# Four block pairs of a first projection by Strassen's seven products, with a ring of eight PSUM banks

## The chip, the core and the metric

The kernel runs on one core of one Trainium2 chip. The metric is the device time of one launch in microseconds (us), median of the runs. PE is TensorE (matmuls), DVE is VectorE, ACT is ScalarE, POOL is GpSimd, SP is the engine that issues most of the stores. PSUM is the memory that PE writes[...]. SBUF is the working memory.

## What is computed

Sparse attention of 8 batches with 8 heads, 576 positions and 64 values a head (four heads see the last 32 positions, four see every 32nd), followed by a bilinear feed-forward part on the 4608 resulting rows of 512 values:

```python
a = x @ w_a                      # 4608 x 512 by 512 x 1536
b = x @ w_b
return (a * b @ w_out)           # 4608 x 1536 by 1536 x 512
```

## The kernel before

Matmuls take bf16 operands and add up in f32. The 4608 rows are cut into nine tiles of 512. `xT` holds the attention output transposed, with the 512 values of a row in `KD` = 4 slices of 128 partitions. The 1536 middle columns are `FD` = 12 blocks of 128.

The work is a list of slots, 16 for each tile. Slots 0 to 11 of a tile are `ffn_ab(t, f)`, the first projection of block f: four matmuls (one per slice, 512 columns each) for `a` and four for `b`, all of them line 581, each group into a PSUM bank of its own. ACT copies `a` to SBUF (line 598), and DVE multiplies it by `b`, which it reads from PSUM, into `pf` (lines 601 and 603). Slots 12 to 15 are the output projection. For tiles 2 to 8 this is already done by Strassen's seven products (`y_plan`, for tile 8 `y_tail`): a two by two block matrix product with seven multiplications in place of eight, for which DVE makes sums of blocks of `pf` beforehand (`fast_s`, lines 614, 616, 618), and sums of blocks of `w_out` once (`fast_w`). The products are the matmuls of lines 686 and 714 (256 columns each). Products that share a bank letter in the plan go into one bank one after the other, the later one added to the earlier one; between them ACT or DVE reads the bank. The last subtraction of each quarter is done by POOL (line 881 for tiles 2 to 7; lines 730 and 735 for tile 8).

The order is written by hand. [...] Attention steps of a later batch lie between the slots of tiles 0 to 6; the last, `V7` of batch 7, is at slot 110. `do(slot, f, ...)` appends work after a slot: loads, `fast_s`, the POOL subtractions, the stores. After a slot that has such work, POOL first makes a one-element copy of that slot's result (`pace`, line 936), which holds POOL's queue back until the slot is done. The sums of a tile's `pf` are spread in this way over the slots of its projection; for tile 8 the sums of pair g (blocks 2g and 2g+1) stand after slot 2g+1.

`mm_bank` hands out PSUM banks in turn. From slot 0 on, the pools are `pst` (two banks, attention scores), `o` (two, attention output), and three `mm` banks with one `tp` bank, which make a ring of four for the projections. Tile 8's output products take the freed `o` and `pst` banks for their second half.

Of the kernel before, what the change touches and what calls it, by code (L numbers as in the profile page):

```python
# [7 lines left out]
F32 = mybir.dt.float32  # L8
BF16 = mybir.dt.bfloat16
I16 = mybir.dt.int16  # L10
ALU = mybir.AluOpType
# [13 lines left out]
VW = 128  # L25
WCH = (0, 2, 5, 9, 12)
FAST_Y = (2, 3, 4, 5, 6, 7, 8)


@with_exitstack  # L30
def kernel(
# [10 lines left out]
    nc = tc.nc  # L42
    B, H, S, D = q.shape
# [5 lines left out]
    KD = d_model // 128  # L49
    FD = d_ff // 128  # L50
    TTOK = 512
    NT = n_tok // TTOK
# [5 lines left out]
    nat = ctx.enter_context(tc.tile_pool(name="nat", bufs=1))  # L58
    sb = ctx.enter_context(tc.tile_pool(name="sb", bufs=3))
    fsb = ctx.enter_context(tc.tile_pool(name="ffn", bufs=2))  # L60
    pst = ctx.enter_context(tc.tile_pool(name="pst", bufs=1, space=bass.MemoryType.PSUM))
    dram = ctx.enter_context(tc.tile_pool(name="dram", bufs=2, space=bass.MemoryType.DRAM))

    psum4 = {}

    def open_psum(stack, **bufs):
        for nm, n in bufs.items():
            psum4[nm] = stack.enter_context(tc.tile_pool(name=f"p{nm}", bufs=n, space=bass.MemoryType.PSUM))
# [7 lines left out]
    def qk_buf(nm):  # L76
        return (const.tile([128, 2, S], BF16, name=f"{nm}l"), const.tile([128, 2, RS * GP], BF16, name=f"{nm}s"))

    qz_buf = [[qk_buf(f"qz{i}{j}") for j in range(2)] for i in range(2)]
    kT_buf = [(const.tile([128, 2, PAD + S], BF16, name=f"kT{i}l"), const.tile([128, 2, RS * GP + 48], BF16, name=f"kT{i}s"))  # L80
              for i in range(2)]
    vl_buf = [const.tile([128, HL * 6, VW], BF16, name=f"vl{i}") for i in range(2)]

    nat_s = {nm: const.tile([128, 3, RS * D], BF16, name=f"nat{nm}") for nm in "qk"}
    p_buf = [const.tile([128, 2, PW], BF16, name=f"p{i}") for i in range(5)]
# [72 lines left out]
    XR = 4  # L158
    xT = const.tile([128, KD, XR * S], BF16)
    wa_sb = wp.tile([128, KD, d_ff], BF16)  # L160
    wb_sb = wp.tile([128, KD, d_ff], BF16)
    wo_sb = wp.tile([128, FD, d_model], BF16)

    FG = FD // 2
    HT = TTOK // 2
    SW = HT + 16
    HN = d_model // 2
# [391 lines left out]
    def take(pos):  # L559
        for b, names in steps.get(pos, ()):  # L560
            run(b, names)

    pfs = {}

    used = [0]

    def mm_bank(shape):
        nm = "tp" if used[0] % 4 == 3 and used[0] >= 0 else "mm"
        used[0] += 1
        return psum4[nm].tile(shape, F32, tag=nm, name="mm")  # L570

    def ab_mm(t, f, ab, kks, mid=None, first=0, last=KD - 1, ws=(0, 1)):
        n = min(TTOK, XR * S - TTOK * t % (XR * S))
        cuts = [(0, n)] + ([(n, TTOK - n)] if n < TTOK else [])
        for w, ps_ in [((wa_sb, wb_sb)[i], ab[i]) for i in ws]:
            if mid and ps_ is ab[1]:
                mid()
            for kk in kks:
                for c0, n in cuts:
                    x0 = (TTOK * t + c0) % (XR * S)  # L580
                    nc.tensor.matmul(ps_[:, c0:c0 + n], lhsT=w[:, kk, 128 * f:128 * (f + 1)], rhs=xT[:, kk, x0:x0 + n],  # L581
                                     start=(kk == first and c0 == 0), stop=(kk == last and c0 == cuts[-1][0]))

    def ffn_ab(t, f, mid, ab=None):
        if f == 0:
            pfs[t] = fsb.tile([128, FD, TTOK], BF16, tag="pf", name="pf", bufs=1)
        pf = pfs[t]
        if ab is None:
            ab = [mm_bank([128, TTOK]) for _ in range(2)]
            if f == 0:  # L590

                late = 1 if t == 1 else 3
                ab_mm(t, f, ab, [kk for kk in range(KD) if kk != late], last=-1)
                ab_mm(t, f, ab, [late], first=-1, last=late)
            else:
                ab_mm(t, f, ab, range(KD), mid)
        a_sb = fsb.tile([128, TTOK], F32, tag="a_sb", name="a_sb")
        nc.scalar.copy(a_sb, ab[0])  # L598
        if t in FAST_Y:
            halves = lambda x: x.rearrange("p (a i s) -> p a i s", i=2, s=16)  # L600
            nc.vector.tensor_mul(pf[:, f, :].rearrange("p (i a s) -> p a i s", i=2, s=16), halves(a_sb), halves(ab[1]))  # L601
        else:
            nc.vector.tensor_mul(pf[:, f, :], a_sb, ab[1])  # L603
        return pf[:1, f, :1]
# [87 lines left out]
    def y_tail(t):  # L692

        plan, y = products(t), y_bufs()
        w, e = f32t("ya"), f32t("ye")
        v = {"a": w, "y": y}
        for q in range(2):
            if q == 0:
                bank = {x: mm_bank([128, HN]) for x in "abcd"}
            else:  # L700
                bank = {"a": psum4["o"].tile([128, 2, 512], F32, tag="o", name="end")[:, 0, :HN],
                        "b": pst.tile([128, 2, 512], F32, tag="st", name="end")[:, 0, :HN],
                        "c": mm_bank([128, HN]), "d": mm_bank([128, HN])}
            c21, c12, c22 = y[1][:, q, col(0)], y[0][:, q, col(1)], y[1][:, q, col(1)]
            wq, eq = w[:, q], e[:, q]
            seen = set()
            for k in ("3415267", "3412567")[q]:
                b, lhs, rhs = plan[k]
                cuts = [(slice(0, HN), bank[b])]
                if (k, q) == ("7", 1):  # L710
                    cuts = [(slice(0, 128), bank[b][:, :128]), (slice(128, HN), mm_bank([128, 128]))]
                for n, dst in cuts:
                    for g in range(FG):
                        nc.tensor.matmul(dst, lhsT=lhs(g, q), rhs=rhs(g)[:, n], start=g == 0 and b not in seen,  # L714
                                         stop=g == FG - 1, skip_group_check=True)
                        if g < FG - 1:
                            yield v
                    if k == "3":
                        nc.scalar.copy(wq, bank["a"])
                    elif k == "4":  # L720
                        nc.vector.tensor_tensor(wq, bank["b"], wq, op=ALU.add)
                        if q == 0:
                            fast_s(t, 1, slice(FG - 1, FG))
                    elif k == "1":
                        nc.vector.tensor_tensor(eq, bank["c"], wq, op=ALU.add)
                        if q == 0:
                            fast_s(t, 2, slice(FG - 1, FG))
                    elif k == "2":
                        nc.scalar.copy(c21, bank["b"])
                        nc.gpsimd.tensor_tensor(wq, wq, c21, op=ALU.subtract)  # L730
                        if q == 1:
                            y_store(nc.sync, t, y, 1, q, col(0))
                    elif k == "5":
                        nc.scalar.copy(c12, bank["a"])
                        nc.gpsimd.tensor_tensor(eq, eq, c12, op=ALU.subtract)
                        if q == 1:
                            y_store(nc.scalar, t, y, 0, q, col(1))
                    elif k == "6":
                        nc.vector.tensor_tensor(c22, bank["c"], wq, op=ALU.add)
                        y_store(nc.sync, t, y, 1, q, col(q) if q else slice(0, d_model))  # L740
                    else:
                        nc.vector.tensor_tensor(y[0][:, q, n], eq[:, n], dst, op=ALU.subtract)
                        if q == 0:
                            y_store(nc.sync, t, y, 0, q)
                        else:
                            y_store(nc.scalar if n.start == 0 else nc.sync, t, y, 0, q, n)
                    yield v
                seen.add(b)
# [48 lines left out]
    with tc.manual_schedule(engines={ENG.PE, ENG.SP, ENG.Pool, ENG.DVE, ENG.Activation}):  # L797
# [30 lines left out]
        for nm in ORDER:  # L828
            if nm[0] == "*":
                spin(int(nm[1:]))  # L830
            elif nm == "C0":
                for x, cp, n in ((raw[0], nc.vector.tensor_copy, "k"), (raw[1], nc.scalar.copy, "q")):
                    t = nats[0, n, False][:, 0:2].rearrange("p h r d -> p (h r d)")
# [21 lines left out]
            elif nm[0] == "F":  # L855
                f = int(nm[1])
# [10 lines left out]
            else:  # L867
                PART[nm[:-2] + nm[-1]](int(nm[-2]))
        early.close()
        open_psum(ctx, mm=3, tp=1, o=1)  # L870
        slots = []
        for t in range(NT):
            slots += [(ffn_ab, t, f) for f in range(FD)] + [(ffn_ys if t in FAST_Y else ffn_y, t, j) for j in range(4)]
# [4 lines left out]
        at = {}  # L878

        def do(i, fn, *args):  # L880
            at.setdefault(i, []).append(lambda: fn(*args))

        soon = {16 * t + 11: [lambda t=t: fast_s(t, 0, slice(2, 6))] for t in FAST_Y[:-1]}
        do(0, fill_v, vl_buf[0])
# [34 lines left out]
            do(slot, fast_w, n, slice(3, 6))  # L919
        for g in range(FG):  # L920
            for n in range(3 if g < FG - 1 else 1):
                do(16 * (NT - 1) + 2 * g + 1, fast_s, NT - 1, n, slice(g, g + 1))
        for t in FAST_Y[:-1]:
            for slot, n, z0, z1 in ((4, 0, 0, 2), (6, 2, 0, 2), (8, 1, 0, 2), (10, 2, 2, 4), (11, 2, 4, 6),
                                    (12, 1, 2, 6)):
                do(16 * t + slot, fast_s, t, n, slice(z0, z1))
        for i, (fn, t, j) in enumerate(slots):
            if i == 0:
                used[0] = -1000 * 3
            elif i == 16:  # L930
                used[0] = 0
            mid = lambda: take(i - 0.5)
            done = fn(t, j, mid) if fn is not ffn_ab else fn(t, j, mid, first.get(j) if t == 0 else None)
            if i > 13 and i in at and done is not None:

                nc.gpsimd.tensor_copy(pace, done)  # L936
            for f in soon.get(i, ()):
                f()
            take(i)
            for f in at.get(i, ()):  # L940
                f()
# [28 lines left out]
```

## Time and profile before

| | |
|---|---|
| device time, median of 3 runs | 328.78 us (328.7 to 328.8) |
| span of the profiled run | 326.3 us, mean PE clock 0.999 |
| tile 7: projection, output products | 262.6 to 283.4, 283.4 to 292.5 us |
| tile 8: projection, output products and end | 292.5 to 313.2, 313.2 to 326.3 us |
| VectorE busy in these four stretches | 10.5 of 20.8, 5.2 of 9.1, 14.2 of 20.7, 4.9 of 13.1 us |
| ScalarE busy in them | 7.0, 1.8, 7.0, 2.2 us |
| GpSimd busy in them | 4.8, 2.4, 3.4, 3.1 us |

The page of a profile gives the busy time of each engine, the span in 40 slices with a digit for each engine (9 is busy for 90% or more), the chain of work that ended last followed back from the end, and groups of instructions by line. A timeline row gives the start in us, the duration in us, engine, line, operation, output and inputs, the shape, and in brackets how long the engine was idle before and what it waited for. A chain row gives start, duration, engine, line and how many instructions in a row.

### The profile page before, as it was taken

Reading aid. Unit: us, or ns where it says so; the run is one execution under the profiler, and the core shown is the slowest. Engines: PE = TensorE matmul, PEld = TensorE weight load, DVE = VectorE, ACT = ScalarE, POOL = GpSimd, SP = SyncE. Lnnn points to the kernel's source line nnn. Section 1 sums busy time; section 2 is a strip of 40 time slices with the busy share of each in tenths; the row PEclk is TensorE's granted clock in tenths of the full one; section 3 lists DMA queues with packets and bytes.
Section 4 is the critical chain, followed back from the end, with each engine's and each line's share of the span. In section 5 each row is a group of like instructions: output and inputs, shape, how many; then the busy total and the mean of one; then the engine's idle time right before and its main releaser. Section 6 shows DMA issues by size and latency. Waiting matters only on the chain.

```text
span 326.3 us, 7676 instructions
## 1 busy us (share of the span) xinstructions
PE 320.6 (98%) x2820; PEld 205.5 (63%) x2820; DVE 265.7 (81%) x509; ACT 202.7 (62%) x329; POOL 177.2 (54%) x295
## 2 busy tenths in 40 slices
PE   8999999999999999999999999999999999999995
PEld 6754655455555587557999985569555954584474
DVE  6766888889778999999999999999877845647562
ACT  6764775478778765777677757875677643313321
POOL 8935839599966655875577557853312031232021
PEclk9999999999999999999999999999999999999999
DMA  9999999999999798799979999898033022004004
GB/s 151 154 204 201 204 184 182 173 171 136 132 213 116 95 97 79 77 217 125 83 72 199 138 86 77 160 180 84 20 77 115 2 67 64 0 2 129 1 2 129
DMA packets 98869, 37.50 MB, mean 115 GB/s; under 512 B 76688, under 2 KB 96016, under 8 KB 98832
## 3 DMA queue, kind: packets, MB, share of 16 engines
q0 software_dynamic: 85968, 19.48, 64.5%
q1 hardware_dynamic: 12576, 17.34, 18.4%
q8 instruction: 22, 0.36, 0.4%
q10 hardware_dynamic: 288, 0.20, 0.2%
q14 instruction: 15, 0.12, 0.1%
HBM read 39.51 MB, written 9.44 MB: 150 GB/s over the span
## 4 chain that ended last, share of the span: by engine, by line
PE 96%; DMA 2%; POOL 0%; DVE 0%; issue 0%; POOLq 0%; ACT 0%; DVEq 0%
PE mm L581 56%; PE mm L686 17%; PE mm L768 6%; PE st L385 5%; PE o L486 4%; DMA shared<-in_q_dram 2%; PE mm L714 2%; PE o L442 1%; PE ab L581 1%; PE misc L154 1%; PE tp L511 1%; PE tp L296 1%; PE end L714 1%; PE tp L287 0%; POOL shared L197 0%
## 5 line engine op out<-in xcount | busy, mean ns | idle before, releaser
L581 PE MATMUL mm<-xT,wa_sb 128*128 128x512 bf16 (+1 forms) x472 | 110.3, 357 | 0.0
L581 PE MATMUL mm<-xT,wb_sb 128*128 128x512 bf16 (+1 forms) x472 | 110.3, 357 | 0.0
L598 ACT COPY a_sb<-mm 128x512 f32<-128x512 f32 x106 | 62.1, 586 | 48.3 <-PE mm L581 47.6
L936 POOL CAST pace<-pf 1x1 f32<-1x1 bf16 x84 | 31.4, 374 | 84.0 <-DVE pf L601 80.7
L581 PEld LDWEIGHTS <-wb_sb 128*128 128x128 bf16 x480 | 46.3, 98 | 44.0 <-issue 0.2
L601 DVE TENSOR_TENSOR pf<-a_sb,mm 128x512 bf16<-128x512 f32 x84 | 56.4, 672 | 17.0 <-PE mm L581 13.8
L581 PEld LDWEIGHTS <-wa_sb 128*128 128x128 bf16 x480 | 42.7, 98 | 31.3
L393 ACT ACTIVATE p<-st 128x576 bf16<-128x576 f32 (+1 forms) x64 | 41.6, 650 | 11.7 <-PE st L385 11.1
L495 ACT ACTIVATE xr<-o 64x576 f32<-64x576 f32 x48 | 31.1, 649 | 25.0 <-PE o L486 24.2
L686 PEld LDWEIGHTS <-ps 128*128 128x128 bf16 x360 | 34.6, 98 | 3.9
L496 ACT ACTIVATE xr<-xr 64x576 f32<-64x576 f32 x48 | 32.9, 685 | 1.5
L500 DVE TENSOR_TENSOR xT<-o,xr 64x288 bf16<-64x288 f32 x48 | 21.5, 447 | 7.2 <-ACT xr L496 6.7
L502 DVE TENSOR_TENSOR xT<-o,xr 64x288 bf16<-64x288 f32 x48 | 21.5, 448 | 6.2 <-ACT xr L496 5.1
L686 PE MATMUL mm<-wf,ps 128*128 128x256 bf16 x216 | 26.4, 273 | 0.0
L768 PE MATMUL mm<-wo_sb,pf 128*128 128x512 bf16 x96 | 23.4, 379 | 0.0
L403 DVE TENSOR_TENSOR p<-p,mask_l 128x576 int16<-128x576 int16 x32 | 22.2, 694 | 1.2 <-ACT p L393 1.1
L243 POOL DMA_DIRECT2D vs<-in_v_dram x24 | 19.7, 821 | 3.0 <-PE st L385 2.2
L212 POOL DMA_DIRECT2D kl<-in_k_dram x24 | 16.1, 671 | 5.5 <-issue 3.6
L212 POOL DMA_DIRECT2D ql<-in_q_dram x24 | 16.0, 666 | 5.2 <-DMA wo_sb<-in_moe_w_out_dram 3.8
L603 DVE TENSOR_TENSOR pf<-a_sb,mm 128x512 bf16<-128x512 f32 x22 | 14.9, 676 | 4.3 <-ACT a_sb L598 2.8
L936 POOL COPY pace<-y_sb 1x1 f32<-1x1 f32 x16 | 2.8, 177 | 27.8 <-ACT y_sb L669 15.1
L686 PE MATMUL mm<-wf,pf 128*128 128x256 bf16 x144 | 17.6, 273 | 0.0
(162 smaller groups left out, 502.1 us busy)
## 6 DMA issues: line engine op xcount, KB each, us to landing
out_dram<-y_sb SPq DMA_DIRECT2D x12, 512.0 KB, 4.6
out_dram<-y_sb SPq DMA_DIRECT2D x10, 256.0 KB, 3.3
vl<-in_v_dram POOLq DMA_DIRECT2D x6, 384.0 KB, 6.8
kl<-in_k_dram POOLq DMA_DIRECT2D x24, 72.0 KB, 3.0
ql<-in_q_dram POOLq DMA_DIRECT2D x24, 72.0 KB, 3.0
vs<-in_v_dram POOLq DMA_DIRECT2D x24, 72.0 KB, 3.7
wo_sb<-in_moe_w_out_dram POOLq DMA_DIRECT2D x4, 384.0 KB, 9.2
natk<-in_k_dram POOLq DMA_DIRECT2D x20, 72.0 KB, 3.3
```

The source lines that it names most:

```text
L212: nc.gpsimd.dma_start(out=t[32 * h:32 * h + 32], in_=src[b, h].rearrange("(i y) d -> y i d", y=32))
L393: nc.scalar.activation(p[:M, :, :W], st[:M, :, :W], ACT.Exp, scale=scale)
L403: nc.vector.tensor_tensor(pi, pi, mk, op=ALU.bitwise_and)
L495: nc.scalar.activation(r, sums, ACT.Ln)
L496: nc.scalar.activation(r, r, ACT.Exp, scale=-1.0)
L500: nc.vector.tensor_mul(dst[:, W * half:W * (half + 1)], o[:64, j, :W], r[:, j])
L581: nc.tensor.matmul(ps_[:, c0:c0 + n], lhsT=w[:, kk, 128 * f:128 * (f + 1)], rhs=xT[:, kk, x0:x0 + n], start=(kk == first and c0 == 0), sto ...
L598: nc.scalar.copy(a_sb, ab[0])
L601: nc.vector.tensor_mul(pf[:, f, :].rearrange("p (i a s) -> p a i s", i=2, s=16), halves(a_sb), halves(ab[1]))
L686: nc.tensor.matmul(bank[b][:, q], lhsT=lhs(g, q), rhs=rhs(g), start=new and q == 0 and g == 0, stop=g == FG - 1, skip_group_check=True)
L768: nc.tensor.matmul(ybank[j], lhsT=pf[:, f, 128 * j:128 * (j + 1)], rhs=wo_sb[:, f], start=(f == 0), stop=(f == FD - 1))
L936: nc.gpsimd.tensor_copy(pace, done)
```

## The change

For the pairs g = 1 and g = 3 (blocks 2 and 3, 6 and 7) of tiles 7 and 8, the factor `a` is computed by Strassen's seven products instead of eight matmuls of 512 columns: the two blocks of a pair, the two halves of the 512 rows (interleaved by 16 rows) and the two halves of the 512 input values make the two by two blocks. The factor `b` stays as it was. The purpose is to have fewer matmul columns.

The sums of blocks of `w_a` (`fast_aw`) are made by VectorE in slots 104 to 110, those of `xT` (`fast_ax`) in slots 111 and 112 for tile 7 and 124 to 127 for tile 8. They and the f32 intermediates lie in buffers of the attention part, which are free by then. Inside a pair PE's order is products 3, 4, 1, 7, the `b` block of the first member, products 2, 5, 6, the `b` block of the second. The two multiplications into `pf` are owed: they are written behind the next block's work.

From tile 7 on (slot 112) the four pools of PSUM end, and one ring of eight banks takes their place; POOL's pacing copies stop there too. In the second half of tile 8's output the last subtractions go from POOL to VectorE, which reads the product from its bank. The sums of tile 8's `pf` are moved to slots 1, 4, 5, 8, 9 and 11.

```diff
+FAST_A = {7: (1, 3), 8: (1, 3)}
...
+    def fast_ax(t, n):
+        (j, i), (j2, i2), op = (((0, 0), (1, 1), ALU.add), ((0, 1), (1, 1), ALU.subtract), ((1, 0), (0, 0), ALU.subtract),
+                                ((0, 0), (0, 1), ALU.add), ((1, 0), (1, 1), ALU.add))[n]
+        nc.vector.tensor_tensor(xsum[t % 2][n].rearrange("p k (a s) -> p k a s", s=16), xhalf(t, j, i), xhalf(t, j2, i2), op=op)
...
+        plan = {"3": ("a", wav[:, 0, 0, g], xs[1]), "4": ("b", wav[:, 1, 1, g], xs[2]), "1": ("c", asum[0][:, g], xs[0]),
+                "7": ("d", asum[4][:, g], xs[4]), "2": ("b", asum[1][:, g], xhalf(t, 0, 0)),
+                "5": ("a", asum[2][:, g], xhalf(t, 1, 1)), "6": ("c", asum[3][:, g], xs[3])}
+        for k in ("3", "4", "1", "7", 0, "2", "5", "6", 1):
+            if k not in plan:
+                bank[k] = direct(2 * g + k)
+                continue
+            b, lhs, rhs = plan[k]
+            new = b not in bank
+            if new:
+                bank[b] = mm_bank([128, HT])
+            for kk in range(2):
+                nc.tensor.matmul(bank[b], lhsT=lhs[:, kk], rhs=rhs[:, kk], start=new and kk == 0, stop=kk == 1,
+                                 skip_group_check=True)
+            if k == "3":
+                nc.scalar.copy(w, bank["a"])
+            elif k == "4":
+                nc.vector.tensor_tensor(w, bank["b"], w, op=ALU.add)
+            elif k == "1":
+                nc.vector.tensor_tensor(v, bank["c"], w, op=ALU.add)
+            elif k == "7":
+                nc.vector.tensor_tensor(v, bank["d"], v, op=ALU.add)
+                while owed:
+                    owed.pop(0)()
+            elif k == "2":
+                nc.scalar.copy(c(1, 0), bank["b"])
+            elif k == "5":
+                nc.scalar.copy(c(0, 1), bank["a"])
+                nc.gpsimd.tensor_tensor(c(0, 0), v, c(0, 1), op=ALU.subtract)
+            else:
+                nc.vector.tensor_tensor(w, bank["c"], w, op=ALU.add)
+                nc.gpsimd.tensor_tensor(c(1, 1), w, c(1, 0), op=ALU.subtract)
+        owed.extend((lambda: product(0), lambda: product(1)))
...
+        if f // 2 in FAST_A.get(t, ()):
+            if f % 2 == 0:
+                fast_a(t, f // 2)
+            return None
+        while owed:
+            owed.pop(0)()
...
                         nc.scalar.copy(c21, bank["b"])
-                        nc.gpsimd.tensor_tensor(wq, wq, c21, op=ALU.subtract)
-                        if q == 1:
+                        if q == 0:
+                            nc.gpsimd.tensor_tensor(wq, wq, c21, op=ALU.subtract)
+                        else:
+                            nc.vector.tensor_tensor(wq, wq, bank["b"], op=ALU.subtract)
                             y_store(nc.sync, t, y, 1, q, col(0))
...
-        open_psum(ctx, mm=3, tp=1, o=1)
+        open_psum(mid_psum, mm=3, tp=1, o=1)
...
-                do(16 * (NT - 1) + 2 * g + 1, fast_s, NT - 1, n, slice(g, g + 1))
+                do(16 * (NT - 1) + (1, 4, 5, 8, 9, 11)[g], fast_s, NT - 1, n, slice(g, g + 1))
...
+        for t, when in ((7, (111, 111, 112, 112, 112)), (8, (124, 125, 126, 127, 127))):
+            for n, slot in enumerate(when):
+                do(slot, fast_ax, t, n)
...
+            elif i == 112:
+                used[0] = -1000 * 3
+                mid_psum.close()
+                open_psum(late_psum, mm=8)
...
-            if i > 13 and i in at and done is not None:
+            if 13 < i < 112 and i in at and done is not None:
```

More of the change, by code (lines that the diff above doesn't have):

```diff
@@ L60 @@
     fsb = ctx.enter_context(tc.tile_pool(name="ffn", bufs=2))
-    pst = ctx.enter_context(tc.tile_pool(name="pst", bufs=1, space=bass.MemoryType.PSUM))
+    mid_psum, late_psum = ctx.enter_context(ExitStack()), ctx.enter_context(ExitStack())
+    pst = mid_psum.enter_context(tc.tile_pool(name="pst", bufs=1, space=bass.MemoryType.PSUM))
     dram = ctx.enter_context(tc.tile_pool(name="dram", bufs=2, space=bass.MemoryType.DRAM))
@@ L582, in ab_mm @@
                                      start=(kk == first and c0 == 0), stop=(kk == last and c0 == cuts[-1][0]))
+    wav = wa_sb.rearrange("p (j k) (g e m) -> p j e g k m", j=2, e=2, m=128)
+    flat = lambda x: x.rearrange("p a b -> p (a b)")
+    asum = [flat(x)[:, 1536 * z:1536 * (z + 1)].rearrange("p (g k m) -> p g k m", g=FG, k=2)
+            for x, z in ((vl_buf[0], 0), (vl_buf[0], 1), (vl_buf[1], 0), (vl_buf[1], 1), (nat_s["k"], 0))]
+    xsum = [[flat(qz_buf[i][x][y])[:, 512 * z:512 * (z + 1)].rearrange("p (k m) -> p k m", k=2)
+             for x, y, z in ((0, 0, 0), (0, 0, 1), (0, 1, 0), (0, 1, 1), (1, 0, 0))] for i in range(2)]
@@ new lines, with xhalf, fast_aw @@
+    scratch = [flat(p)[:, :2 * HT].bitcast(F32) for p in p_buf[:4]]
+    def xhalf(t, j, i):
+        x0 = TTOK * t % (XR * S)
+        return xT[:, 2 * j:2 * j + 2, x0:x0 + TTOK].rearrange("p k (a i s) -> p i k a s", i=2, s=16)[:, i]
+    def fast_aw(n, gs):
+        (j, e), (j2, e2), op = (((0, 0), (1, 1), ALU.add), ((0, 1), (1, 1), ALU.add), ((0, 0), (1, 0), ALU.add),
+                                ((0, 1), (0, 0), ALU.subtract), ((1, 0), (1, 1), ALU.subtract))[n]
+        nc.vector.tensor_tensor(asum[n][:, gs], wav[:, j, e, gs], wav[:, j2, e2, gs], op=op)
@@ new lines, in fast_ax, with fast_a, direct, product @@
+    def fast_ax(t, n):
+        (j, i), (j2, i2), op = (((0, 0), (1, 1), ALU.add), ((0, 1), (1, 1), ALU.subtract), ((1, 0), (0, 0), ALU.subtract),
+                                ((0, 0), (0, 1), ALU.add), ((1, 0), (1, 1), ALU.add))[n]
+        nc.vector.tensor_tensor(xsum[t % 2][n].rearrange("p k (a s) -> p k a s", s=16), xhalf(t, j, i), xhalf(t, j2, i2), op=op)
+    owed = []
+    def fast_a(t, g):
+        pf, xs = pfs[t], xsum[t % 2]
+        a = [flat(x)[:, :2 * TTOK].bitcast(F32) for x in kT_buf[g % 2]]
+        c = lambda e, i: a[e][:, HT * i:HT * (i + 1)]
+        w, v = scratch[2 * (g % 2)], scratch[2 * (g % 2) + 1]
+        bank = {}
+        def direct(f):
+            b = mm_bank([128, TTOK])
+            x0 = TTOK * t % (XR * S)
+            for kk in range(KD):
+                nc.tensor.matmul(b, lhsT=wb_sb[:, kk, 128 * f:128 * (f + 1)], rhs=xT[:, kk, x0:x0 + TTOK], start=kk == 0,
+                                 stop=kk == KD - 1)
+            return b
+        def product(e):
+            f, b = 2 * g + e, bank[e]
+            nc.vector.tensor_mul(pf[:, f, :].rearrange("p (i a s) -> p i a s", i=2, s=16),
+                                 a[e].rearrange("p (i a s) -> p i a s", i=2, s=16),
+                                 b.rearrange("p (a i s) -> p i a s", i=2, s=16))
+        plan = {"3": ("a", wav[:, 0, 0, g], xs[1]), "4": ("b", wav[:, 1, 1, g], xs[2]), "1": ("c", asum[0][:, g], xs[0]),
[31 more added lines that the diff above has]
+        owed.extend((lambda: product(0), lambda: product(1)))
@@ L697, in y_tail @@
         for q in range(2):
[L698 to L703, printed above, removed]
+            bank = {x: mm_bank([128, HN]) for x in "abcd"}
             c21, c12, c22 = y[1][:, q, col(0)], y[0][:, q, col(1)], y[1][:, q, col(1)]
@@ L734, in y_tail @@
                         nc.scalar.copy(c12, bank["a"])
-                        nc.gpsimd.tensor_tensor(eq, eq, c12, op=ALU.subtract)
-                        if q == 1:
+                        if q == 0:
+                            nc.gpsimd.tensor_tensor(eq, eq, c12, op=ALU.subtract)
+                        else:
+                            nc.vector.tensor_tensor(eq, eq, bank["a"], op=ALU.subtract)
                             y_store(nc.scalar, t, y, 0, q, col(1))
@@ L926 @@
                 do(16 * t + slot, fast_s, t, n, slice(z0, z1))
+        for slot, n, g in ((104, 0, 1), (104, 1, 1), (105, 2, 1), (105, 3, 1), (106, 4, 1), (107, 0, 3), (108, 1, 3), (109, 2, 3), (109, 3, 3), (110, 4, 3)):
+            do(slot, fast_aw, n, slice(g, g + 1))
+        for t, when in ((7, (111, 111, 112, 112, 112)), (8, (124, 125, 126, 127, 127))):
+            for n, slot in enumerate(when):
+                do(slot, fast_ax, t, n)
         for i, (fn, t, j) in enumerate(slots):
```

## The prediction

> **What bounds the kernel now.** I read the page first: busy shares, slices, then the chain that ended last.
>
> ```profile
> PE 320.6 (98%) x2820; PEld 205.5 (63%) x2820; DVE 265.7 (81%) x509; ACT 202.7 (62%) x329; POOL 177.2 (54%) x295
> PE   8999999999999999999999999999999999999995
> PE 96%; DMA 2%; POOL 0%; DVE 0%; issue 0%; POOLq 0%; ACT 0%; DVEq 0%
> ```
>
> PE is busy in every slice but the last, and 96% of the chain is PE. A busy PE need not be PE at its peak, so I asked next for PE's waits from 232 us to the end (the answer has no row) and for the chain in order of time over the end:
>
> ```profile
> 283.36 9.17 PE mm L686 x84
> 292.52 20.72 PE mm L581 x96
> ...
> 320.58 0.38 ACT y_sb L729
> 320.96 0.07 issue
> 321.03 0.73 POOL ya L730
> 321.76 0.70 POOLq L965
> 322.45 0.02 issue
> 322.48 0.29 DVE y_sb L742
> ```
>
> The first projection of tile 8 is 96 matmuls of 512 columns in 20.72 us, **0.2158 us each**; the output products of tile 7 are 84 of 256 columns in 9.17 us, **0.1092 us each**. Both stream without a gap. Hence any matmul time saved in tiles 7 and 8 comes off the end, and any wait put in front of a matmul there is added. Only the last part, from 320.55 us, is a chain of copies, subtractions and stores.
>
> So the question is whether the helpers keep up. The VectorE timeline at the start of tile 8 shows how its queue runs:
>
> ```profile
> 296.09 0.69 DVE L601 TENSOR_TENSOR pf<-a_sb,mm 128x512 bf16<-128x512 f32 x1 [0.65 <-PE mm L581]
> 296.81 0.29 DVE L614 TENSOR_TENSOR ps<-pf 128x256 bf16<-128x256 bf16 x1
> 297.02 1.62 DVE L616 TENSOR_TENSOR ps<-pf 128x512 bf16<-128x512 bf16 x1
> 298.56 0.41 DVE L618 TENSOR_TENSOR ps<-pf 128x512 bf16<-128x512 bf16 x1
> ...
> 300.26 0.29 DVE L614 TENSOR_TENSOR ps<-pf 128x256 bf16<-128x256 bf16 x1
> 300.47 0.42 DVE L616 TENSOR_TENSOR ps<-pf 128x512 bf16<-128x512 bf16 x1
> 300.81 0.42 DVE L618 TENSOR_TENSOR ps<-pf 128x512 bf16<-128x512 bf16 x1
> 301.27 0.69 DVE L601 TENSOR_TENSOR pf<-a_sb,mm 128x512 bf16<-128x512 f32 x1
> ```
>
> It runs in written order: the product of a block, three sums of the same block pair (0.97 us in all), then the next product. The third row takes 1.62 us instead of 0.42. In the POOL timeline its neighbour is
>
> ```profile
> 297.10 1.26 POOL L881 TENSOR_TENSOR y_sb<-ya,y_sb 128x512 f32<-128x512 f32 x1
> ```
>
> which ends at 298.36, just before the VectorE sum does. Today this delay hides: block f's banks are wanted again only two blocks later.
>
> [...] 1.62 against 0.42 us above, while L601, with a PSUM input, ran its usual 0.69 us at 267.92 beside L881 (267.16 to 268.42). [...] 512 elements take 0.42 us at L618 and 0.69 us at L662. [...]
>
> **The matmuls.** A pair's first factor is 8 matmuls of 512 columns, 8 x 0.2158 = 1.727 us. Seven products of 2 matmuls of 256 columns are 14 x 0.1092 = 1.528 us. Saved 0.198 us a pair, **0.79 us for four**. Weight loads (98 ns in the page) stay shorter than a matmul, as in L686. Products 2 and 5 read xT in runs of 16 elements, which no row shows on the moving side: between 0.109 us and, as an estimate, twice that; I take 0.109.
>
> **Helpers per pair.** ScalarE loses two copies of 0.586 and gets three of 0.373: nothing. POOL gets two subtractions of 0.73 us, as in L730. VectorE keeps both products (0.69) and gets four adds of the L721 kind, 0.42 each, +1.7 us. It is busy 10.5 of 20.8 us in tile 7's projection and 14.2 of 20.7 in tile 8's, so the total fits; the order is what matters. The ten weight sums in tile 6 (0.29 us each, L614's size) come where VectorE idles 0.8 to 0.9 us every second block and banks have over 1.5 us of slack: nothing. Tile 8's five activation sums fall beside tile 7's output products, where VectorE is busy 5.2 of 9.1 us: nothing.
>
> **The new wait inside a pair.** Let T be PE's start of a pair. It runs products 3, 4, 1, 7 (0.87 us), the four L581 matmuls of the second factor (0.86), then product 2 at T+1.74 *into product 4's bank*. That must wait until VectorE's add "4" has read the bank, and this add queues behind everything written before the pair. The product of the preceding block cannot start before T+0.28 (296.09 against the next block's first matmul at 295.81). Tile 7's second pair has only that ahead of it: add "4" runs T+0.95 to T+1.37; no wait. In tile 8 the sums of pair 0 (slot 1) and pair 2 (slot 5) stand between. In the rows above: 0.72 to the first sum, +0.21, +0.34, +0.46 to the next instruction: add "4" starts at T+0.28+1.73 = T+2.01, ends T+2.44; with 0.05 for the signal PE resumes at T+2.49 against T+1.74: **0.75 us, in both pairs, 1.5 us**. Add "1", 0.34 later, is in time for product 6. Queued behind product 2 on PE is everything to the end.
>
> **The start of tile 7.** Two things meet. First, four PSUM pools end and one pool of eight banks begins at slot 112. Whether its first tile waits for its own bank (free) or for the last reader of all the old pools is not in the page; that reader is
>
> ```profile
> 262.74 0.69 DVE L675 TENSOR_TENSOR ya<-mm,ya 128x512 f32<-128x512 f32 x1
> ```
>
> ending 263.43, while PE would start at 262.47: 0 or 1.0 us. Second, VectorE must make five activation sums (0.42 us each if at the double rate[...]; 0.69 if not): two behind L675, three behind the first block's product. L881 holds the SBUF side from 262.64 to 263.90, and without the pacing copies its second run follows at once. POOL slipped in between two VectorE sums at 297.10, so I let it do so again: sum 0 ends 264.3, POOL 265.6, sum 1 266.0, product 0 266.7, sums 2 to 4 267.8, product 1 268.5, add "4" 268.92. If PE waited 1.0 us at the pool change, the pair starts at 266.92; product 7 wants the last sum at 267.58 and gets it at 267.85, product 2 then follows without more than 0.05: 1.3 us in all. If it did not wait there, the pair starts at 265.92, product 7 at 266.58 waits 1.25, and the total is again **1.3 us**. Bounds: 0.1 (own bank, POOL does not slip in) to 2.4 (sums at the single rate, four of them 0.27 longer).
>
> **The end.** With POOL out, the last chain is ScalarE's copies to 320.95 and 321.60, VectorE's subtractions (0.42) ending 322.05, c22 at 322.39, and the last two cuts, set by PE's end near 322.5. The last cut ends about 0.1 us earlier: **-0.1**. The freed banks change nothing else: no row waits for one.
>
> Sum: 328.78 - 0.79 - 0.1 + 1.5 + 1.3 = **330.7 us**.
>
> **Rivals.** (1) The start of tile 7 costs 0.1: 329.4. For it: the wait for other banks is not needed by the data. Against it: VectorE's five sums sit there in any case. (2) Nothing waits: 327.9, faster. For it: VectorE has room in every stretch, PE has no wait today. Against it: room on average doesn't help an add standing behind 1.73 us of earlier work with 1.46 us (T+0.28 to T+1.74) to go, its own 0.42 included. (3) The sums run at the single rate (+1.1 us), 331.8; or the moving operand in short runs costs double, 16 x 0.109 = 1.7 us more, 332.4. Against: the double rate was seen on sliced bf16 operands.
>
> **Chances.** Forecast 0.55, (1) 0.17, (2) 0.15, (3) 0.13. 0.2% is 0.66 us: the band of no change ends at 329.44, so I give most of (1) to it and the rest to slower: faster 0.15, same 0.13, slower 0.72. The range from 329.1 to 331.8 leaves out (2) and the far half of (3).
>
> **What would show it.** PE waits on VectorE at product 2 in tile 8, twice some 0.75 us, absent in tile 7's second pair; a PE wait of about 1 us at slot 112 for L675, or of about 1.2 us at product 7 for the last activation sum; 14 matmuls of a pair in 1.53 us when nothing holds them; activation sums of 0.42 us. The forecast is wrong if PE shows no waits there, which would need add "4" to run ahead of the sums, or if it waits in other places, such as on products late behind POOL.

## The result, and the profile after

| | before | changed |
|---|---|---|
| device time, median of 6 runs each | 328.69 us (328.07 to 328.80) | 331.97 us (330.78 to 334.16) |
| ratio, 95% interval | | 1.0108 (1.0070 to 1.0147) |
| the profiled run: time, span | 328.46, 326.3 us | 330.78, 329.1 us |

The change makes the kernel slower, by more than forecast: 331.97 us lies just above the range. The profiled run is the quickest of the six; of the others, three had a mean granted PE clock of 0.989 to 0.994 (1.000 is full speed) in place of 0.999 and took 332.6 to 334.2 us. So two things need explaining: 2.3 us in the profile, and the spread above it.

The page of the changed kernel (lines as in the page before):

```profile
PE 318.5 (97%) x2810; PEld 207.6 (63%) x2844; DVE 279.1 (85%) x547; ACT 201.9 (61%) x333; POOL 176.8 (54%) x286
PE 91%; DVE 4%; issue 2%; DMA 1%; ACT 1%; SPq 0%; DVEq 0%
```

PE's share of the chain fell from 96 to 91%; VectorE has 4%. PE's waits from 225 us to the end, of which there were none before (engine, line, what it waited for: us in total, times, longest):

```profile
PE mm L583 <- DVE ya L763: 2.1, 1, 2.1
PE mm L644 <- DVE p L649: 0.9, 2, 0.4
```

The first is at slot 112. The timeline of all engines there, with a weight sum of the usual length ahead of it:

```profile
257.76 0.28 DVE L601 TENSOR_TENSOR vl<-wa_sb 128x256 bf16<-128x256 bf16 x1
...
262.57 1.25 POOL L968 TENSOR_TENSOR y_sb<-ye,y_sb 128x512 f32<-128x512 f32 x1
262.67 1.30 DVE L601 TENSOR_TENSOR natk<-wa_sb 128x256 bf16<-128x256 bf16 x1
...
263.90 0.68 DVE L763 TENSOR_TENSOR ya<-mm,ya 128x512 f32<-128x512 f32 x1
...
264.63 0.82 PE L583 MATMUL mm<-xT,wa_sb 128*128 128x512 bf16 x2 [2.06 <-DVE ya L763]
```

L763 is the old L675, the last reader of an old bank. It started 1.16 us later than before, because a weight sum (L601, slot 110) stood ahead of it and took 1.30 us instead of 0.28: it has two SBUF inputs, lay beside POOL's subtraction L968 (262.57 to 263.82) and ended 0.15 us after it. In the profile of the kernel before, all seven VectorE instructions with two SBUF inputs that lay beside L881 ended 0.28 to 0.33 us after it (six of L403, 128x576 int16, took 1.47 to 2.25 us at a median of 0.45 for that shape; the seventh is the sum of 1.62 us), while the seven with a PSUM input of 512 columns took 0.65 to 0.69 us. In the kernel before, PE's row at this place was

```profile
262.47 0.81 PE L581 MATMUL mm<-xT,wa_sb 128*128 128x512 bf16 x3
```

The second is in tile 8, at product 2 of each pair. VectorE and PE in the first of them:

```profile
297.60 0.38 PE L644 MATMUL mm<-qz00l,wa_sb 128*128 128x256 bf16 x2
...
297.87 0.69 DVE L689 TENSOR_TENSOR pf<-a_sb,mm 128x512 bf16<-128x512 f32 x1 [0.49 <-PE mm L583]
...
298.59 0.29 DVE L702 TENSOR_TENSOR ps<-pf 128x256 bf16<-128x256 bf16 x1
298.80 0.42 DVE L704 TENSOR_TENSOR ps<-pf 128x512 bf16<-128x512 bf16 x1
299.13 0.42 DVE L706 TENSOR_TENSOR ps<-pf 128x512 bf16<-128x512 bf16 x1
299.47 0.41 DVE L649 TENSOR_TENSOR p<-mm,p 128x256 f32<-128x256 f32 x1
299.94 0.60 PE L644 MATMUL mm<-xT,vl 128*128 128x256 bf16 x4 [0.44 <-DVE p L649]
```

This is the queue of the prediction, step by step: product of the preceding block, three sums, add "4", then PE. The pair began at 297.60 (first row), so product 2 came at T+2.34, not at T+1.74.

Where the 2.3 us are, from the starts of stages in both timelines: tile 7 starts 2.16 us later (262.47, 264.63); its projection is 0.38 us shorter (20.72, 20.34); from there to the start of tile 8's output, 0.99 us longer (29.89, 30.88), which is 0.38 saved and two times 0.69 waited (a pair took 3.94 instead of 3.25 us: 0.60 more up to product 2, 0.09 more from there to product 6); then 0.12 us less to the end of the last VectorE instruction, 0.15 more from there to the end of the span, where the last stores are. Sum +2.80, the change of the span. The device time rose by 2.32 only, since what lies outside the span fell from 2.16 to 1.68 us.

### The profile page after: what moved, and what is told of

Its sections match the earlier page's. It is cut to its first block, busy times and chain, and to the rows that moved or that the text cites. A ratio compares the mean times of both kernels' runs of the same rounds, so it can differ in the third digit from the quotient of the medians.

```text
span 329.1 us, 7734 instructions
## 1 busy us (share of the span) xinstructions
PE 318.5 (97%) x2810; PEld 207.6 (63%) x2844; DVE 279.1 (85%) x547; ACT 201.9 (61%) x333; POOL 176.8 (54%) x286
## 4 chain that ended last, share of the span: by engine, by line
PE 91%; DVE 4%; issue 2%; DMA 1%; ACT 1%; SPq 0%; DVEq 0%
PE mm L583 49%; PE mm L774 16%; PE mm L855 6%; PE st L387 5%; PE o L488 4%; PE mm L797 2%; PE mm L622 2%; PE mm L644 1%; PE o L444 1%; DMA raw<-in_q_dram 1%; PE ab L583 1%; PE misc L156 1%; PE tp L513 1%; PE tp L298 1%; DVE pf L689 1%
## 5 line engine op out<-in xcount | busy, mean ns | idle before, releaser
L583 PE MATMUL mm<-xT,wa_sb 128*128 128x512 bf16 (+1 forms) x419 | 100.2, 355 | 3.2 <-DVE ya L763 2.1
L583 PE MATMUL mm<-xT,wb_sb 128*128 128x512 bf16 (+1 forms) x431 | 100.8, 355 | 0.2
L686 ACT COPY a_sb<-mm 128x512 f32<-128x512 f32 x98 | 57.4, 586 | 43.1 <-PE mm L583 42.2
L583 PEld LDWEIGHTS <-wb_sb 128*128 128x128 bf16 x448 | 43.2, 98 | 40.2 <-issue 0.2
L583 PEld LDWEIGHTS <-wa_sb 128*128 128x128 bf16 x448 | 39.5, 98 | 29.8 <-DVE ya L763 2.3
L689 DVE TENSOR_TENSOR pf<-a_sb,mm 128x512 bf16<-128x512 f32 x76 | 50.9, 670 | 5.9 <-PE mm L583 5.0
L1032 POOL CAST pace<-pf 1x1 f32<-1x1 bf16 x70 | 27.6, 394 | 48.9 <-DVE pf L689 45.7
L691 DVE TENSOR_TENSOR pf<-a_sb,mm 128x512 bf16<-128x512 f32 x22 | 14.9, 676 | 4.2 <-ACT a_sb L686 2.6
L774 PE MATMUL mm<-wo_sb,ps 128*128 128x256 bf16 x144 | 17.5, 273 | 0.0
```

The costliest lines, as they stand in the source:

```text
L774: nc.tensor.matmul(bank[b][:, q], lhsT=lhs(g, q), rhs=rhs(g), start=new and q == 0 and g == 0, stop=g == FG - 1, skip_group_check=True)
```

## The experiments

Theory: all of the loss is PE waiting for VectorE, in two places, and the spread comes from a drop of PE's clock after the longer wait. Rivals are named with each run. Runs measured together share a chip and their runs of the kernel before, so each is set against the 328.8 to 329.1 us that the kernel before took there.

**Own-bank waits.**

```diff
-psum4[nm] = stack.enter_context(tc.tile_pool(name=f"p{nm}", bufs=n, space=bass.MemoryType.PSUM))
+psum4[nm] = stack.enter_context(tc.tile_pool(name=f"p{nm}", bufs=n, space=bass.MemoryType.PSUM, reuse_waits=waits))
...
-open_psum(late_psum, mm=8)
+open_psum(late_psum, waits="tile", mm=8)
```

> The changed kernel, with each tile of the new ring waiting only for the last reader of its own bank. Theory (the 2.2 us at slot 112 are a wait for readers of other banks, and behind it VectorE's queue would hold product 7 anyway): the wait at slot 112 goes, a wait of about 1.6 us appears in tile 7's first pair for the last activation sum, and the profiled time falls by about 0.5 us, from 330.8 to 330.3. Rival (the wait at slot 112 is the whole cost at the start of tile 7): it falls by 2 us, to 328.7. On the spread of the executions (330.8 to 334.2 us, with a granted clock of 0.999 to 0.989): if one PE wait of over 2 us brings the clock down, the spread gets smaller here.

Measured: 330.08 us (329.83 to 330.47, clock 1.000 in 5 of 5), against 328.87 before. The profiled execution took 329.83 us. PE's waits now, and below them the timeline row of product 7:

```profile
PE mm L644 <- DVE p L649: 0.9, 2, 0.4
PE mm L644 <- DVE qz10s L606: 0.6, 1, 0.6
PE mm L644 <- DVE qz10l L606: 0.4, 1, 0.4
...
267.78 0.38 PE L644 MATMUL mm<-qz11l,natk 128*128 128x256 bf16 x2
```

The wait at slot 112 is gone, and waits for activation sums took its place, at the first two products of tile 7's first pair and less at product 7: its matmuls start at 267.78 us, 1.46 us after their turn (the pair's turn was 265.66, product 7 comes 0.66 later). From one profiled execution to the other (330.78 to 329.83) the time fell by 0.95 us, nearer to the theory's 0.5 than to the rival's 2. By the timelines 0.77 us of it is the difference of the two waits: 2.23 us from PE's turn at 262.40 in the changed kernel, 1.46 here. Another 0.19 us lies ahead of slot 112, where this run's turn came at 262.21. (The turns are worked out from the last twelve products of tile 6, begun at 261.09 and 260.90, at 0.109 us each.) VectorE's queue, not the pool change alone, sets the start of tile 7.

**Tile 8's sums behind the adds.**

```diff
-do(16 * (NT - 1) + (1, 4, 5, 8, 9, 11)[g], fast_s, NT - 1, n, slice(g, g + 1))
+do(16 * (NT - 1) + (2, 4, 6, 8, 9, 11)[g], fast_s, NT - 1, n, slice(g, g + 1))
```

> The changed kernel, with the sums of tile 8's pairs 0 and 2 written one slot later, behind the adds of the pair that follows (slots 2, 4, 6, 8, 9, 11). Theory (add 4 stands behind three sums on VectorE and holds product 2): both PE waits in tile 8 go, 0.69 us each, and the profiled time falls by 1.4 us to 329.4; the wait at slot 112 stays at 2.2 us, and so does the spread of the executions. Rival (product 2 waits for something else, such as ScalarE or the bank ring): the waits stay, 330.8.

Measured: ten executions in two groups, 329.47 to 330.15 us at a clock of 0.999 or 1.000, and 331.26 to 331.69 at 0.995, five in each; median 330.70. PE has one wait left:

```profile
PE mm L583 <- DVE ya L763: 2.1, 1, 2.1
```

The profiled run took 329.61 us, 1.2 less than that of the changed kernel (1.4 expected). The cause of tile 8's waits is shown: moving sums, with nothing else changed, removes both. The spread stays with the wait of 2.1 us.

**The pool change alone** (in the kernel before). The ring also gives `y_tail` its banks, as in the changed kernel.

```diff
+            elif i == 112:
+                used[0] = -1000 * 3
+                mid_psum.close()
+                open_psum(late_psum, mm=8)
```

> The kernel before with one thing added: from slot 112 on one ring of eight banks in place of the four pools (no Strassen in the first projection, pacing and last subtractions as before). Theory (the first tile of the new pool waits for the last reader of any old bank, the subtraction L675, which ended 1.0 us after PE was ready): PE waits 1.0 us at slot 112 and the time rises by 1.0 us to 329.7. Rival (no such wait; the 2.2 us come from VectorE's new sums alone): 328.7. If a PE wait of this length brought the clock down, executions of 330 us and over would show too.

Measured: 329.78 us (329.43 to 330.14, 11 executions), +0.9 us over 328.87; ratio 1.0024 (1.0016 to 1.0033).

```profile
262.92 0.69 DVE L676 TENSOR_TENSOR ya<-mm,ya 128x512 f32<-128x512 f32 x1
263.66 0.82 PE L582 MATMUL mm<-xT,wa_sb 128*128 128x512 bf16 x2 [0.85 <-DVE ya L676]
```

PE starts 0.05 us after the last reader of any old bank has ended, as the theory has it, and no execution shows a drop.

**All three mended.** Besides the two edits above:

```diff
-((104, 0, 1), (104, 1, 1), (105, 2, 1), (105, 3, 1), (106, 4, 1), (107, 0, 3), (108, 1, 3), (109, 2, 3), (109, 3, 3), (110, 4, 3))
+((98, 0, 1), (100, 1, 1), (101, 4, 1), (102, 0, 3), (103, 1, 3), (104, 2, 1), (105, 3, 1), (106, 2, 3), (107, 3, 3), (108, 4, 3))
...
-(7, (111, 111, 112, 112, 112))
+(7, (112, 111, 111, 110, 112))
...
-do(16 * t + 15, nc.gpsimd.tensor_tensor, y[0][:, :, col(0)], v["e"], y[0][:, :, col(1)], ALU.subtract)
+do(16 * t + (14 if t == 6 else 15), nc.gpsimd.tensor_tensor, y[0][:, :, col(0)], v["e"], y[0][:, :, col(1)], ALU.subtract)
...
-if 13 < i < 112 and i in at and done is not None:
+if 13 < i < 114 and i in at and done is not None:
```

> The changed kernel with all three things mended: own-bank waits; tile 8's sums as in the run before last; the weight sums 2 to 7 slots earlier (none after slot 108), one activation sum of tile 7 at slot 110, two at 111, two at 112, POOL's first subtraction of tile 6 one slot earlier and its second held back until slot 113. Theory (PE time saved is real and all of the loss is waits on VectorE): no PE wait over 0.2 us in tiles 7 and 8, time 328.7 - 0.76 - 0.1 = 327.8 us, clock 0.999 in every execution. Rival (VectorE's 1.7 us more per pair hold PE wherever they are put): 329 us or more.

Measured: **327.58 us** (327.21 to 327.77) against 328.87; ratio 0.9957 (0.9945 to 0.9969). This version beats both kernels. PE has no wait left in tiles 7 and 8. The chain through tile 8's first pair (start, us, engine, line, count):

```profile
295.35 0.87 PE mm L644 x8
296.22 0.86 PE mm L622 x4
297.09 0.65 PE mm L644 x6
297.74 0.86 PE mm L622 x4
```

Eight and six matmuls of 256 columns in 0.87 and 0.65 us: the seven products in 1.52 us, 0.109 us a matmul as in L686 before. Only tile 8's second pair still loses some 0.25 us. The mean clock was 1.000 in four executions and 0.997 in one.

**Without the sum at slot 110.**

```diff
-(109, 3, 3), (110, 4, 3))
+(109, 3, 3), (106, 4, 3))
```

> The changed kernel with one edit: the weight sum of slot 110 stands at slot 106. Theory (this sum, shut out by POOL's subtraction until 263.90, stands ahead of the subtraction that the new pool waits for, and makes a 1.0 us wait a 2.1 us one): PE's wait at slot 112 is 0.9 to 1.0 us, with up to 0.3 us at product 7 behind it, and the profiled time is 0.8 to 1.1 us lower, 329.8. Theory on the spread (a wait of about 2 us lets the granted clock drop for a stretch, one of 1 us doesn't): no execution over 330.5 us, clock 0.999 or 1.000. Rival (the clock drops whatever the waits, from the Strassen products): executions of 331.5 us and more stay.

Measured: 329.83 us (329.64 to 330.27). PE's waits and the reader that it waits for:

```profile
PE mm L644 <- DVE p L649: 0.9, 2, 0.4
PE mm L583 <- DVE ya L763: 0.9, 1, 0.9
...
262.94 0.69 DVE L763 TENSOR_TENSOR ya<-mm,ya 128x512 f32<-128x512 f32 x1
```

The wait at slot 112 is 0.9 us in place of 2.1. One sum of 0.28 us had cost about 1 us and, through the clock, more. The waits in tile 8 stay as in the changed kernel, and still no execution is over 330.3.

**The pool change and one unused sum** (in the kernel before).

```diff
+do(110, nc.vector.tensor_tensor, dead[:, :256].rearrange("p (k m) -> p k m", k=2), wa_sb[:, 2:4, 768:896], wa_sb[:, 2:4, 896:1024], ALU.add)
```

> The kernel before with the new ring from slot 112 on, as in the third run, and one weight sum of 128x256 bf16 on VectorE at slot 110, whose result nothing uses; no Strassen in the first projection. Theory: the sum waits for POOL's subtraction, PE waits 2.0 to 2.2 us at slot 112, the lower executions take 330.9 us (1.1 over the third run), and about half of the executions show a clock of 0.995 and take 1.7 to 1.9 us more. Rival (the sum costs its 0.3 us only): 330.1 us, and no drop.

Measured: 331.24 and 331.49 us at a clock of 1.000; 332.39, 332.68 and 332.75 at 0.994 or 0.995; 334.12 at 0.988. PE's wait is 2.1 us, and the sum took 1.32 us:

```profile
262.85 1.32 DVE L877 TENSOR_TENSOR natk<-wa_sb 128x256 bf16<-128x256 bf16 x1
```

The profile fell on an execution at 0.994, and shows where the clock goes. Stretches behind the wait (us; busy time and count of PE, PEld, DVE, ACT, POOL; granted clock; DMA share; GB/s), and the chain:

```profile
264.60:265.10 0.50, 0.27 (x2) 0.16 (x3) 0.17 (x1) 0.00 (x0) 0.00 (x0) 0.99 0.00 0
265.10:268.50 3.40, 3.40 (x10) 1.20 (x9) 0.03 (x1) 0.58 (x1) 0.00 (x0) 0.50 0.58 154
268.50:270.00 1.50, 1.50 (x9) 0.67 (x8) 0.66 (x1) 0.58 (x1) 0.00 (x0) 1.00 0.00 0
```

```profile
264.78 0.05 issue
264.83 22.58 PE mm L582 x96
```

PE resumed at 264.83. Some 0.3 us later the clock fell to 0.50, stayed there for 3.4 us, and came back. The 96 matmuls took 22.58 us; behind the shorter wait of the run with one fill (below), with no drop there, they took 20.89. The drop cost the difference, 1.69 us, which is half of 3.4. Without it the profiled execution would have taken 330.7 us, near the 330.9 expected. The two executions at full clock were 0.3 to 0.6 us above expectation; neither was profiled, and the reason stays open.

**The pool change and three fills** (in the kernel before): a longer wait without a held sum.

```diff
+        for x in dead:
+            do(110, nc.vector.memset, x, 1.0)
```

> The kernel before with the new ring from slot 112 on, and three fills of 570 f32 values a partition on VectorE at slot 110 into dead buffers; no Strassen in the first projection. The fills take about 0.65 us each, as an estimate 1.9 us, some of it in VectorE's idle time, so PE waits 2.3 to 2.8 us at slot 112 without any contention between VectorE and POOL. If the clock depends on the length of the wait alone, more executions than in the run with one sum show it lower, with the same loss of 1.7 to 1.9 us for each drop; if it is tied to the contention, none does.

Measured: PE's wait 2.6 us; six executions, 331.27 and 331.73 us at 1.000 and 0.998, 332.52 to 333.38 at 0.993 to 0.995, one of 336.26 at 0.985. The three fills took 0.53 us each (0.65 expected), the ones beside POOL's subtraction no longer than the last, which was not. So a held sum is not needed: behind this wait of 2.6 us, too, the clock was lower in 4 of 6. More executions with a lower clock than in the run with one sum had been expected; it was as many in both, and six executions can't tell. In the profile the clock is again 0.50 for 3.4 us, here from 267.1 to 270.5 us (the last row is one of the chain):

```profile
265.60:267.10 1.50, 1.32 (x7) 0.61 (x8) 0.12 (x1) 0.00 (x0) 0.00 (x0) 1.00 0.93 197
267.15:270.50 3.35, 3.35 (x10) 1.11 (x9) 0.69 (x1) 1.17 (x2) 0.00 (x0) 0.50 0.16 62
...
265.78 22.58 PE mm L582 x96
```

Here it fell 1.3 us after PE had resumed, and the 96 matmuls took 22.58 us as well.

**The pool change and one fill.** The same with one fill of 520 values.

> The kernel before with the new ring from slot 112 on and one fill of 520 f32 values a partition on VectorE at slot 110 into a dead buffer; no Strassen in the first projection. It lies between the third run (PE wait 0.9 us, clock whole in 11 of 11 executions) and the run with one sum (2.1 us, clock lower in 4 of 6). The fill takes about 0.6 us, so PE waits 1.3 to 1.5 us at slot 112 and the executions without a drop take 330.2 us. If the drop sets in near 2 us, none of them shows a lower clock; if its chance grows in proportion to the wait, about a third do and take 1.8 us more.

Measured, on another chip: PE's wait 1.3 us, 330.26 us against 329.07 before; a clock of 0.994 or less in 3 of 22 executions, where the kernel before, with no such wait, had it in 3 of 35. The profile fell on one of the three, and its drop is elsewhere. The clock rows of this page and of the page of the run with one sum:

```profile
PEclk9959999999999999999999999999999999999999
```

```profile
PEclk9999999999999999999999999999999979999999
```

And this run's chain behind its wait:

```profile
267.66 20.89 PE mm L582 x96
```

In the first row the drop is at some 20 us (0.50 from 17.8 to 24.6 us, twice 3.4), far from the wait, and the 96 matmuls behind the wait took 20.89 us. What let the clock fall there stays open; in that profile PE had waited 0.8 us for a load until 15.0 us, which it had not in the profile of the kernel before. A chance in proportion to the wait, which asks for some 7 of 22, does not fit: at 1.3 us the wait adds no drops that can be told from those of this chip.

**The last subtractions on VectorE** (in the kernel before).

```diff
-                        nc.gpsimd.tensor_tensor(wq, wq, c21, op=ALU.subtract)
-                        if q == 1:
+                        if q == 0:
+                            nc.gpsimd.tensor_tensor(wq, wq, c21, op=ALU.subtract)
+                        else:
+                            nc.vector.tensor_tensor(wq, wq, bank["b"], op=ALU.subtract)
```

> The kernel before with one thing changed: the last subtractions of tile 8's second half on VectorE. In the profiles the device time exceeds the span by 2.1 us where POOL does them and by 1.7 us where VectorE does. Theory (POOL's late work itself costs about 0.45 us beyond the span): the span falls by 0.1 us and the time by 0.5 us, to 328.3. Rival (the difference comes from elsewhere in the change): time and span fall alike by 0.1 us, to 328.8.

Inconclusive. The medians are 328.47 and 328.84 us, but the ratio is 0.9997 (0.9986 to 1.0009). Time outside the span: 1.8 to 2.0 us, against 2.1 to 2.2. It is not POOL's doing alone: the runs with one sum and with fills keep POOL's subtractions and have 1.7 us. What sets it stays open.

**Own banks and moved sums, without the rest** (the changed kernel with the first two edits).

> The changed kernel with two of the three mended things: own-bank waits, and tile 8's sums behind the adds of the pair. The weight and activation sums and POOL's subtractions stay where the change put them. Theory (the waits are independent): the two PE waits of 0.35 and 0.56 us in tile 7's first pair stay, those of tile 8 go, and the time is 330.1 - 1.4 = 328.7 us; so the placing of the sums and of POOL's work is worth the remaining 1.1 us to the version with all three. Rival (one wait only hides another): 329.3 us or more.

Measured, on the chip of the run with one fill: 329.18 us against 329.07; ratio 0.9996 (0.9978 to 1.0014). PE waits 0.6 and 0.4 us for the activation sums, the waits in tile 8 are gone. So the waits are independent, as the theory has it. The time doesn't decide: it is 0.1 us over the kernel before, the theory had 0.2 under it (328.7 against 328.87) and the rival 0.4 over, and the interval holds both. As an estimate from two ratios on two chips, the placing of sums and POOL's work is worth 0.39% (0.9996 to 0.9957), 1.3 us, give or take 0.7.

**The clock, over all runs.** Executions with a mean clock of 0.995 or less: with a PE wait of 2.1 us or more, 3 of 6 (changed kernel), 5 of 10 (tile 8's sums moved), 4 of 6 (one sum) and 4 of 6 (three fills), together 16 of 28 (15 of 27 without the slowest, at 336.26 us). With no single wait above 1.3 us: none of 40 in five runs, 2 of 22 (subtractions on VectorE) and 3 of 22 (one fill); in the kernel before 0 of 21, 0 of 27 and 3 of 35. All versions of the changed kernel without the long wait are among the 40, so the Strassen products alone do not bring it. Where the drop lies was seen in two of the 16 only, those of the run with one sum and of the run with three fills, each time behind the wait; no such execution of the changed kernel was profiled, and for the other 14 the place is inferred from how often it comes. In the run with tile 8's sums moved, the two groups lie 1.8 us apart (means 331.49 and 329.71). As an estimate, one stretch of 3.4 us at half clock takes 0.005 off a mean over 330 us: 0.993 to 0.995 fits one stretch, and 0.985 to 0.990 two or three.

## Why the prediction was wrong

- **Seven products save 0.79 us: right.** Tile 7's projection, in which no pair waited, took 0.38 us less, so 0.76 for four pairs; the moving operand in runs of 16 cost nothing extra (products 2, 5 and 6 took 0.65 us for six matmuls in the run with all three mended, 0.109 each), and the activation sums took 0.42 us where nothing blocked them, so rival (3) did not happen. What the forecast calls the double rate is, in the kernel before, 0.13 us for 256 more columns in bf16 (0.29 us at L614, 0.42 at L618) against 0.27 in f32 with a PSUM input (0.42 at L721, 0.69 at L662).
- **Two waits of 0.75 us in tile 8: right**, 0.69 us lost each time. PE's row at 299.94 starts 0.06 us after add "4", the reader of the bank, ends at 299.88. Add "4" followed the last sum after 0.34 us, not 0.46. The run with moved sums shows that the sums were the cause.
- **No wait in tile 7's second pair: right.** Its product 2 came at its turn (276.55 for a pair begun at 274.81, T+1.74).
- **The start of tile 7, 1.3 us: the cause is right, the size wrong, 2.2 us.** The term that failed is "The ten weight sums in tile 6 (...): nothing". I judged them by idle time on average and by bank slack. The last of them, at slot 110, met POOL's subtraction and stood ahead of the very instruction that the pool change waits for. I knew both facts, the sum of 1.62 us beside POOL and the reader L675, and did not put the sums into the queue between them. With that sum moved away the wait is 0.9 us, near the 1.0 forecast. The 0.3 us at product 7 did not come: the longer pool wait let VectorE catch up.
- **The end, -0.1 us: right up to the last VectorE instruction** (-0.12), but the last stores took 0.15 us more, so that the span gained nothing. The 0.48 us outside the span was not foreseen and is not explained; it made up for part of the error above, so that the profiled run lies at 330.78 beside the 330.7 forecast. That agreement is luck.
- **The spread: no term for it at all.** "Any wait put in front of a matmul there is added" is too little for a long wait. Behind 2.1 us the clock was lower in about half of the executions, at 1.7 us for a stretch. The three at 0.999 lie at 330.78, 330.88 and 331.35 us, inside the range; the other three lift the median to 331.97, out of it. With the wait at the predicted 1.0 us (the run without the sum at slot 110) no execution shows it.
- **A slip in the sums:** rival (1), with 0.1 in place of 1.3 us, comes to 329.5 us, not 329.4. Nothing above hangs on it.

## What to carry to other kernels

Where one engine is the bound, a helper's spare time on average says little: write down, for each wait, what stands ahead of the awaited instruction in its queue, and whether one of these can be held up by another engine, as the sum of 1.30 us was. Small preparatory sums belong behind the instruction that the bound engine waits for, or well ahead of it: one slot later was enough for tile 8's sums, four slots earlier for the last weight sum. When buffer pools change owner on the critical path, ask whether the first user waits for its own buffer or for all readers of the old ones.

## What the runs showed of the hardware beyond expectation

A PE wait of 2.1 to 2.6 us can cost more than its length. In the two profiles that caught it, the granted clock fell to 0.50 within 0.3 and 1.3 us of PE's return, for 3.4 us, at a cost of 1.7 us; by the mean clocks some drop came in 16 of 28 executions with such waits. After waits of 0.9 and 1.3 us lower clocks were no more frequent, as far as 38 executions can tell, than in the kernel before on the same chips. The VectorE sum that took 1.30 us in place of 0.28 beside POOL's subtraction also put off the instruction behind it, by 1.16 us. That one has a PSUM input, and beside POOL it was no longer: in the run with the pool change alone it took its usual 0.69 us, from 262.92, beside a POOL subtraction from 262.82 to 264.08.
